# Halving the chunk of a state space kernel: from 128 tokens per tile to two chunks of 64 on the partitions of one

## The chip, the cores and the metric

The kernel runs on one core of a Trainium2 chip. The metric is the device time of one execution in microseconds (us); the figure compared is the median of several executions. Profile times are counted from the start of the profiled execution's span.

The engines are called PE (TensorE matmul), PEld (TensorE weight load, which overlaps PE), DVE (VectorE), ACT (ScalarE), POOL (GpSimd) and SP (the engine that issues most of the DMAs). "L623" is line 623 of the kernel whose profile is shown.

## The reference

Two stages. First a state space layer (Mamba-2 form) over 4 batches, 8 heads, 768 tokens, 32 features per head and a state of 16: the tokens are cut into chunks, inside a chunk the output is a masked and decayed matrix product, and between chunks a state is carried. Then a two-layer MLP with a PReLU over the 3072 tokens x 256 features, with 2048 hidden features. All in fp32 (the weights come as 64-bit floats and are converted on the chip).

```python
for c in range(nc):                                   # chunks of 32 tokens in the reference
    ...                                               # xc, Bc, Cc, la: this chunk's x, B, C, log a
    cum = np.cumsum(la, axis=-1)
    L = np.exp(cum[..., :, None] - cum[..., None, :]) * causal
    CB = np.einsum('bhin,bhjn->bhij', Cc, Bc)         # the gram
    y_intra = np.einsum('bhij,bhjd->bhid', CB * L, xc)            # "within" the chunk
    y_inter = np.einsum('bhin,bhnd->bhid', Cc, state) * np.exp(cum)[..., None]   # "across"
    y[:, :, sl] = y_intra + y_inter
    Bx = Bc (outer) xc * exp(cum_last - cum)
    state = decay_full * state + sum_j Bx             # what the chunk adds to the state
...
h = x @ w_in                                          # 3072x256 @ 256x2048
g = np.maximum(h, 0.0) + alpha * np.minimum(h, 0.0)
out = g @ w_out                                       # 3072x2048 @ 2048x256
```

The result does not depend on the chunk's length, so a kernel is free to choose it. The MLP's products are done with a seven-product block scheme (Strassen-Winograd) for all tokens but the first 512.

## The kernel before

There are 24 chunks of 128 tokens, taken two at a time: 12 "pairs". A pair is a Python generator that is advanced stage by stage between matmuls of the MLP of the token group before; two pairs make one group of 512 tokens. Every matmul's `tile_position` names the part of the 128x128 array that it uses; the numbers of rows (contraction) and columns (outputs) are those of its operands.

```python
P = 128; Q = 128                      # partitions; tokens in a chunk
...
def spread(z, k, tile=...):           # pairs 0 and 1: decays of a head to all partitions, by matmul
    ts = [tile(w) for w in range(2)]
    for q in range(4):
        for w in range(2):
            ...
            nc.tensor.matmul(ts[w][:, q * Q : (q + 1) * Q],
                             ident[rs, row : row + 1].to_broadcast([64, P]), z[rs, k], ...,
                             tile_position=(64 * w, 0))
...
def load_spread(gp, b, c):            # later pairs: the same by DMA, from a scratch in DRAM
    for k, t in enumerate(loads["p", gp][1]):          # two tiles abc, 128 x (8 heads x 128)
        rows = scratch["z", b // 2]....[b % 2, c + k]
        nc.sync.dma_start(out=t..., in_=rows.unsqueeze(0).to_broadcast([P, H, Q]))
```

The stages of a pair (cut; `k` is the chunk, `w` the half of the heads, `h` a head, `r` a group of 32 partitions of B and C, which is two heads):

```python
for i in range(2):                    # B and C turned, 4 transposes of 128x128
    for k in range(2):
        nc.tensor.transpose(tp[...], nat[:, i, k], ident)
...                                   # copied to bh and ct by ACT; cz: C with every second head zeroed
# decays inside a chunk: a scan along the row, for each of 128 start tokens
def half_decays(k, w):
    for i in range(2):                # 8 scans of 128x256 for a pair
        nc.vector.tensor_tensor_scan(out=dv[:, k, hs], data0=abc[k][:, hs],
                                     data1=ident_p[0], ...)
# pairs 0 and 1: 4 scans of 128x512 that read spread's result in PSUM
...
# what a chunk adds to the state, and the states
for k in range(nk):                   # nk = 2; 1 in the last pair of a batch
    for w in range(KC):
        nc.tensor.matmul(dps[ws, k], bn[:, k, ws], xt[:, k, w * P : (w + 1) * P],
                         tile_position=(0, 64 * w), ...)             # 128x64 of the array
for k in range(nk):
    nc.vector.scalar_tensor_tensor(out=new[:, k], in0=old, scalar=pf[...], in1=dps[:, k], ...)
...
# gram of B and C
for k in range(2):
    for r in range(4):
        nc.tensor.matmul(gram[r][:, k], bh[rs, k], cz[rs, :, k],
                         tile_position=(32 * r, 0), ...)             # 32x128, 256 columns stream
...
for r in ...:                         # times the decays: 4 of 128x512 on DVE
    nc.vector.tensor_tensor(out=dec[:, :, hs], in0=gram[r], in1=dec[:, :, hs], op=ALU.mult)
# the outputs: across (from the states) and within (from the chunk), summed in PSUM
for k in range(2):
    for w in range(KC):
        nc.tensor.matmul(y[w][:, k], st[k][ws], cd[ws, k], start=not begun, stop=False,
                         tile_position=(64 * w, 0), ...)             # 64x128, 128 columns stream
for k in range(2):
    for w in range(KC):
        for q in range(4):
            nc.tensor.matmul(y[w][32 * q : 32 * q + 32, k], xt[:, k, h * D : (h + 1) * D],
                             dec[:, k, h], start=False, stop=True,
                             tile_position=(0, 32 * q), ...)         # 128x32, 128 columns stream
for w in range(KC):
    nc.scalar.copy(out=xts[g][:, w, ...], in_=y[w]...)               # xT, the input of the MLP
```

The start (cut): the weights are loaded in 16 pieces (`raw`) and converted by ACT, POOL and DVE (`convert_a`, `convert_b`, `convert`), and the first two pairs have no MLP to hide behind.

```python
load_next(2); rows_clamp(0); ssm(0)
held["pr"] = rows_scan(0); rows_out(0)
load_pair(1); load_second(); load_next(2); load_pair(2, False); load_next(2)
load_spread(2, ...)
ssm(0); convert_a(*pieces[0]); ssm(0); convert_b(*pieces[0]); ssm(0)
convert_a(*pieces[1]); ssm(1); convert_next(halves=(nc.vector, nc.gpsimd)); ssm(0); ssm(1)
slopes(alpha)
prelus = [hidden_two(0, 0, 0, spare())]
convert_a(*pieces[2]); convert_next(first=False); ssm(1); convert_a(*pieces[3])
prelus.append(hidden_two(0, 2, 0, spare()))
for rest in prelus: rest()
convert_next(); ssm(1); convert_next(first=False)
...                                   # 4 hidden blocks of the other 256 tokens, then f = 4 to 15:
for f in range(FIRST, NF):            # pairs 2 and 3 in between, weights converted along the way
    ...
    hidden(0, f); convert_next(); output(f - FIRST)
```

Of the kernel before, what the change touches and what calls it, by code (L numbers as in the profile page):

```python
# [22 lines left out]
def kernel(  # L23
# [32 lines left out]
    P = 128  # L56
    Q = 128
    CPB = S // Q
# [27 lines left out]
    lda = ctx.enter_context(tc.tile_pool(name="lda", bufs=3))  # L86
# [45 lines left out]
    def load_spread(gp, b, c):  # L132

        for k, t in enumerate(loads["p", gp][1]):
            rows = scratch["z", b // 2].rearrange("(b h c) t -> b c h t", b=2, h=H)[b % 2, c + k]
            nc.sync.dma_start(out=t.rearrange("p (h t) -> p h t", h=H),
                              in_=rows.unsqueeze(0).to_broadcast([P, H, Q]))

    def load_pair(gp, decays=True):
# [18 lines left out]
        abc = []  # L158
# [8 lines left out]
        for k in range(2 if gp >= NB else 0):  # L167
            abc.append(lda.tile([P, H * Q], F32, name="abc"))
        loads["p", gp] = nat, abc, xt, ap
        if decays:  # L170
            load_spread(gp, b, c)
# [95 lines left out]
    def keep_warm(to, n, cols=2 * Q):  # L267

        for i in range(n):
# [6 lines left out]
    ident_h = const.tile([P, H * Q], F32, name="ident_h")  # L276
    nc.vector.tensor_copy(out=ident_h.rearrange("p (h t) -> p h t", h=H),
                          in_=ident.unsqueeze(1).to_broadcast([P, H, Q]))
# [13 lines left out]
    zeros = const.tile([P, Q], F32, name="zeros")  # L292
    nc.gpsimd.memset(zeros, 0.0)
    ends = const.tile([P, Q], F32, name="ends")
    nc.vector.memset(ends, 0.0)
    nc.vector.memset(ends[:, Q - 1 :], 1.0)
# [46 lines left out]
    def rows_scan(i):  # L343

        d0 = held[i]
        nc.vector.memset(d0[:, Q:], 0.0)
        pr = prep.tile([RW, Q], F32, name="pr")
        nc.vector.tensor_tensor_scan(out=pr[:, ::-1], data0=d0[:, 1:][:, ::-1],
                                     data1=ends[:RW, ::-1], initial=0.0,
                                     op0=ALU.mult, op1=ALU.add)  # L350
        return pr

    def rows_out(i):
# [4 lines left out]
        nc.vector.tensor_tensor_scan(out=rpf, data0=d0, data1=zeros[:RW], initial=1.0,  # L358
                                     op0=ALU.mult, op1=ALU.add)
        nc.vector.memset(d0[:, :1], 0.0)  # L360
        for key, t in (("z", d0), ("pf", rpf)):
            scratch[key, i] = dr.tile([RW, Q], F32, name=f"{key}{i}")
            nc.sync.dma_start(out=scratch[key, i], in_=t)

    def rows_turn(i, pr):
# [6 lines left out]
        nc.scalar.copy(out=t, in_=ps[:, :RW])  # L372
        if i == 0:
            nc.scalar.copy(out=alpha, in_=ps[:, RW : RW + NF])
        prt[i] = t
        return ps
# [15 lines left out]
    def first_a(ap, eng):  # L392

        z = prep.tile([P, 2, Q], F32, name="z", bufs=2)
        eng.tensor_scalar(out=z.rearrange("p k t -> p (k t)"), in0=ap, scalar1=1e-6,
                          scalar2=1.0, op0=ALU.max, op1=ALU.min)
        eng.memset(z[:, :, :1], 0.0)
        return z

    def spread(z, k, tile=lambda w: ss_tile()):  # L400

        ts = [tile(w) for w in range(2)]
        for q in range(4):
            for w in range(2):
                rs = slice(64 * w, 64 * w + 64)
                row = 64 * w + N * q
                nc.tensor.matmul(ts[w][:, q * Q : (q + 1) * Q],
                                 ident[rs, row : row + 1].to_broadcast([64, P]), z[rs, k],
                                 start=(q == 0), stop=True, tile_position=(64 * w, 0),
                                 skip_group_check=True)  # L410
        return ts
# [5 lines left out]
    def pair(gp):  # L417
# [4 lines left out]
        dec = work.tile([P, 2, H, Q], F32, name="dec")  # L422
        dv = dec.rearrange("p k h t -> p k (h t)")

        def decays(k):

            if abc:
                for w in range(2):
                    half_decays(k, w)
                return  # L430
            for w, t in enumerate(ahead.pop(k, None) or spread(z, k)):
                ws = slice(512 * w, 512 * w + 512)
                nc.vector.tensor_tensor_scan(out=dv[:, k, ws], data0=t, data1=ident_h[:, ws],
                                             initial=0.0, op0=ALU.mult, op1=ALU.add)

        def half_decays(k, w):
            for i in range(2):
                hs = slice((2 * w + i) * 2 * Q, (2 * w + i + 1) * 2 * Q)
                nc.vector.tensor_tensor_scan(out=dv[:, k, hs], data0=abc[k][:, hs],  # L439
                                             data1=ident_p[0], initial=0.0, op0=ALU.mult,  # L440
                                             op1=ALU.add)

        ahead = {}

        pf = ap
        if gp == 0:
            z = first_a(ap, nc.vector)
            ahead[0] = spread(z, 0)
            ahead[1] = spread(z, 1, bank)
            loads["z", 1] = first_a(loads["a", 1], nc.gpsimd)  # L450
            yield
            nc.vector.tensor_scalar(out=ap, in0=ap, scalar1=1e-6, scalar2=1.0, op0=ALU.max,
                                    op1=ALU.min)
            pf = prep.tile([P, 2 * Q], F32, name="pf")
            for k in range(2):
                ks = slice(k * Q, (k + 1) * Q)
                nc.vector.tensor_tensor_scan(out=pf[:, ks], data0=ap[:, ks], data1=zeros,
                                             initial=1.0, op0=ALU.mult, op1=ALU.add)
        elif not abc:
            z = loads.pop(("z", gp))  # L460
            ahead[0] = spread(z, 0, bank)
# [16 lines left out]
        def spread_c():  # L478
            for e in range(2):
                o = cz[:, e].rearrange("p k t -> p (k t)")  # L480
                if gp == 0 and e == 1:
                    nc.gpsimd.tensor_scalar(out=o, in0=ct, scalar1=par[:, e : e + 1],
                                            scalar2=None, op0=ALU.mult)
                else:
                    nc.scalar.mul(o, ct, par[:, e : e + 1])
# [5 lines left out]
        fine = gp >= 2 * GC // 2  # L491
        if not fine:
            spread_c()
        if gp == 0:
            keep_warm(rows_turn(0, held.pop("pr"))[:, HT:], 5, Q)
            yield
        bn = bns.pop(gp) if gp in bns else pair_loads(gp)
        if gp == 1:
            c_decayed()
            dps = spare()  # L500
            ahead[1] = spread(z, 1, lambda w: ss_tile())
        elif gp:
            yield

        if fine:
            for k in range(2):
                for w in range(2):
                    half_decays(k, w)
                    if k == 1 and w == 1:
                        spread_c()  # L510
                    yield
        else:
            decays(0)
            if gp:
                yield
            if gp != 1:
                decays(1)
# [4 lines left out]
        nk = 1 if last else 2  # L522
        st = [masked.get(b)]
        new = work.tile([P, 2, P], F32, name="state")
        sm = work.tile([P, 2, P], F32, name="sm")

        def added(dps):
            dps = dps.rearrange("p (k m) -> p k m", m=P)
            for k in range(nk):
                for w in range(KC):  # L530
                    ws = slice(64 * w, 64 * w + 64)
                    nc.tensor.matmul(dps[ws, k], bn[:, k, ws], xt[:, k, w * P : (w + 1) * P],  # L532
                                     start=True, stop=True, tile_position=(0, 64 * w),
# [542 lines left out]
```

## Time and profile before

The median is 378.76 us (three executions, 378.55 to 379.11); the profiled execution's span is 377.2 us, at a mean granted PE clock of 0.994.

| what, from the table of instruction groups | count | busy us |
|---|---|---|
| L741 and L766: matmuls of the MLP's seven-product part, 128x256 | 1120 | 287.2 in all |
| L561: gram (three rows: into ss, hp and bank) | 192 | 34.1 |
| L616: across, 64x128 | 80 | 10.1 |
| L623: within, 128x32 | 384 | 15.2 |
| L439: scans of later pairs on DVE, 128x256 | 80 | 48.0 |
| L433: scans of pairs 0 and 1, 128x512 | 8 | 9.4 |
| L600: decays times gram, 128x512 | 46 | 30.0 |
| abc<-z: DMAs of 512 KB, 4.9 us from issue to landing | 20 | |

How to read it: a busy time is the time in which at least one instruction of that group ran, so for PE, whose instructions overlap, it is no sum of durations, and the time a group holds the array is better read from where the next group starts in the timeline. Each fp32 matmul of the program shows as two records with a weight load each. A wait is put down to the engine whose signal came last. The granted clock is 0.8 of full speed in the second of 40 slices of the span, and 0.9 or more in all others.

### The profile page before, as it was taken

What the parts mean: (1) busy time and instruction counts of PE and PEld (TensorE: products, weight loads), DVE (VectorE), ACT (ScalarE), POOL (GpSimd) and SP (SyncE); (2) the same over time, 40 slices, a digit from 0 to 9 for tenths busy, and PEclk for the clock granted to TensorE, in tenths of its full rate; (3) what the DMA queues carried; (4) which work ended last, traced back from release to release, by engine and by line L of the source; (5) the groups of instructions that cost most, each with busy time, mean ns of one, the idle gap of its engine ahead of it and who ended that gap; (6) DMA issues with size and microseconds to landing.
All of it is one profiled execution on the core that took longest, in us unless ns stands there. A gap on an engine that the chain in (4) does not pass through costs nothing.

```text
span 377.2 us, 6178 instructions
## 1 busy us (share of the span) xinstructions
PE 367.2 (97%) x2223; PEld 295.5 (78%) x2223; DVE 241.5 (64%) x461; ACT 179.5 (48%) x384; POOL 203.2 (54%) x212
## 2 busy tenths in 40 slices
PE   7999999999999999999999999999999999999996
PEld 6767566668778788788788788888788788888884
DVE  7777699967636737747737847647856734543364
ACT  1466756525344445545435535525625525543541
POOL 4764476679766846445456345356364355254512
PEclk9899999999999999999999999999999999999999
DMA  7999697921008901001901901901711000001003
GB/s 141 186 225 346 162 272 171 180 70 56 30 0 156 179 2 54 5 0 30 180 3 30 179 2 29 180 2 28 140 44 21 9 0 15 17 0 30 1 0 83
DMA packets 121878, 30.71 MB, mean 81 GB/s; under 512 B 93736, under 2 KB 117752, under 8 KB 121848
## 3 DMA queue, kind: packets, MB, share of 16 engines
q1 hardware_dynamic: 116736, 29.74, 35.4%
q10 hardware_dynamic: 5112, 0.59, 1.1%
q8 instruction: 17, 0.28, 0.3%
q14 instruction: 13, 0.11, 0.1%
HBM read 26.98 MB, written 3.34 MB: 80 GB/s over the span
## 4 chain that ended last, share of the span: by engine, by line
PE 84%; DVE 5%; SPq 4%; DMA 2%; ACT 2%; issue 1%; ACTq 0%; POOLq 0%; DVEq 0%
PE hp L766 33%; PE bank L741 32%; PE bank L680 5%; PE hp L642 3%; PE ss L623 2%; PE ss L561 2%; SPq L165 2%; SPq L163 1%; DMA raw<-in_moe_w_in_dram 1%; PE ss L616 1%; DVE dec L439 1%; PE ss L532 1%; DMA nat<-in_B_dram 1%; PE hp L561 1%; PE hp L657 1%
## 5 line engine op out<-in xcount | busy, mean ns | idle before, releaser
L809 POOL TENSOR_TENSOR gt<-gt 128x512 f32<-128x512 f32 x58 | 73.6, 1270 | 31.8 <-DVE gt L751 24.8
L751 DVE SCALAR_TENSOR_TENSOR gt<-hp,s_mul,gt 128x256 f32<-128x256 f32 x120 | 52.5, 479 | 47.8 <-ACT gt L749 46.8
L741 PE MATMUL bank<-gt,w_out 128*128 128x256 f32 x320 | 82.5, 382 | 0.4 <-ACT o_sb L687 0.4
L749 ACT ACTIVATE gt<-hp,s_alpha 128x256 f32<-128x256 f32 x120 | 50.3, 470 | 47.2 <-PE hp L766 32.9
L741 PEld LDWEIGHTS bank<-gt,w_out 128*128 128x128 f32 x320 | 60.0, 190 | 11.2 <-issue 2.3
L800 POOL TENSOR_TENSOR gt<-gt 128x512 f32<-128x512 f32 x20 | 25.4, 1270 | 78.3 <-DVE gt L751 78.3
L741 PE MATMUL bank<-gt,ws 128*128 128x256 f32 x240 | 58.3, 379 | 0.0
L741 PEld LDWEIGHTS bank<-gt,ws 128*128 128x128 f32 x240 | 45.1, 190 | 5.8
L439 DVE TENSOR_TENSOR_SCAN dec<-abc,bank 128x256 f32<-128x256 f32 x80 | 48.0, 660 | 0.0
L766 PE MATMUL hp<-xs,w_in 128*128 128x256 f32 x160 | 42.9, 390 | 0.0
L766 PE MATMUL hp<-xT,w_in 128*128 128x256 f32 x160 | 41.9, 384 | 0.0
L766 PE MATMUL hp<-xs,ws 128*128 128x256 f32 x160 | 41.1, 379 | 0.0
L785 DVE TENSOR_TENSOR hp<-hp,u 128x512 f32<-128x512 f32 x20 | 14.0, 700 | 39.7 <-ACT u L783 39.7
L774 ACT COPY m<-hp 128x512 f32<-128x512 f32 x20 | 11.7, 586 | 51.5 <-PE hp L766 51.5
L766 PEld LDWEIGHTS hp<-xs,w_in 128*128 128x128 f32 x160 | 28.7, 189 | 7.7 <-issue 3.3
L766 PEld LDWEIGHTS hp<-xs,ws 128*128 128x128 f32 x160 | 30.4, 190 | 4.1
L766 PEld LDWEIGHTS hp<-xT,w_in 128*128 128x128 f32 x160 | 29.7, 190 | 5.0 <-issue 1.4
L680 PEld LDWEIGHTS bank<-w_out,gt 128*128 128x128 f32 x128 | 24.2, 190 | 9.6 <-issue 5.4
L680 PE MATMUL bank<-w_out,gt 128*128 128x256 f32 x128 | 30.6, 381 | 0.6 <-POOL w_out L261 0.6
L789 DVE TENSOR_TENSOR c<-hp,m 128x512 f32<-128x512 f32 x20 | 13.6, 681 | 19.3 <-PE hp L766 19.3
L642 PE MATMUL hp<-xT,w_in 128*128 128x512 f32 x48 | 23.2, 605 | 0.0
L783 ACT COPY u<-hp 128x512 f32<-128x512 f32 x20 | 11.7, 585 | 23.0 <-PE hp L766 23.0
(155 smaller groups left out, 557.1 us busy)
## 6 DMA issues: line engine op xcount, KB each, us to landing
abc<-z SPq DMA_DIRECT2D x20, 512.0 KB, 4.9
raw<-in_moe_w_in_dram SPq DMA_DIRECT2D x8, 512.0 KB, 5.5
raw<-in_moe_w_out_dram SPq DMA_DIRECT2D x8, 512.0 KB, 6.8
xt<-in_x_dram SPq DMA_DIRECT2D x24, 128.0 KB, 3.3
out_dram<-o_sb SPq DMA_DIRECT2D x32, 64.0 KB, 1.9
nat<-in_B_dram SPq DMA_DIRECT2D x22, 64.0 KB, 2.7
nat<-in_C_dram SPq DMA_DIRECT2D x22, 64.0 KB, 3.5
ap<-pf SPq DMA_DIRECT2D x11, 128.0 KB
```

Of the source, the lines that this page charges most:

```text
L439: nc.vector.tensor_tensor_scan(out=dv[:, k, hs], data0=abc[k][:, hs], data1=ident_p[0], initial=0.0, op0=ALU.mult, op1=ALU.add)
L642: nc.tensor.matmul(hp, w_in[:, k, f * P : (f + 1) * P], xts[g][:, k], start=(k == 0), stop=(k == KC - 1))
L680: nc.tensor.matmul(pos[0][t // 2][:, t % 2], gt[:, t * Q : (t + 1) * Q], w_out[:, f], start=(f == 0 and t % 2 == 0), stop=(f == NF - 1), s ...
L741: nc.tensor.matmul(ms[g][i][:, h], w, blocks[g, z][n][:, p], start=(q == 0 and h == 0), stop=(q == NQ - 1), skip_group_check=True)
L749: nc.scalar.mul(o[:, p], h[:, p], s_alpha[:, fs[p]])
L751: nc.vector.scalar_tensor_tensor(out=o[:, p], in0=h[:, p], scalar=s_mul[:, fs[p]], in1=o[:, p], op0=ALU.mult, op1=ALU.max)
L766: nc.tensor.matmul(to[:, p], w(2 * z + p), b, start=start and p == 0, stop=True, skip_group_check=True)
L774: nc.scalar.copy(out=m1, in_=A)
L785: nc.vector.tensor_tensor(out=Y, in0=Y, in1=u2, op=ALU.add)
L789: nc.vector.tensor_tensor(out=c22, in0=A, in1=m5, op=ALU.add)
L800: nc.gpsimd.tensor_tensor(out=tc_, in0=g22, in1=g12, op=ALU.subtract)
L809: eng.tensor_tensor(out=o, in0=x0, in1=x1, op=ALU.subtract)
```

## The change

A chunk becomes 64 tokens long (`L`), and two chunks (`e` = 0, 1) lie on the 128 partitions of a tile, so a pair of tiles now holds four chunks. What was one 128x128 block of decays and gram per head and tile becomes two blocks of 64x64, one above the other: half of the elements. The gram then uses 32x64 parts of the array and the within products 64x32 parts, eight at a time instead of four; there are four states per pair instead of two. Across and within no longer sum in PSUM: within is copied by ACT, and DVE adds across to it. The decays of later pairs are loaded as one DMA of 256 KB per tile with runs of 2 KB, and their scans halve. The start is ordered anew, pairs 0 and 1 lose an ACT copy and a POOL product, and piece 0 of the weights is finished on DVE alone.

```diff
+    L = Q // 2
 def load_spread(gp, b, c):
-        for k, t in enumerate(loads["p", gp][1]):
-            ...
-            nc.sync.dma_start(out=t..., in_=rows.unsqueeze(0).to_broadcast([P, H, Q]))
+        t = loads["p", gp][1]
+        for k in range(2):
+            rows = scratch["z", b // 2].rearrange("(c e) x -> c e x", e=2)[c + k]
+            rows = rows[:, b % 2 * H * L : (b % 2 + 1) * H * L]
+            nc.sync.dma_start(out=t[:, k], in_=rows.unsqueeze(1).to_broadcast([2, L, H * L]))
 def spread(z, ...):                                  # 64x64 parts, 64 columns, both chunks at once
+        for i in range(8):
+            for e in range(2):
+                for w in range(2):
+                    nc.tensor.matmul(ts[w][es, i * L : (i + 1) * L], ...,
+                                     tile_position=(64 * w, e * L))
 def half_decays(k, w):                               # 4 scans of 128x256 for a pair
-            for i in range(2):
-                nc.vector.tensor_tensor_scan(out=dv[:, k, hs], data0=abc[k][:, hs], ...)
+            nc.vector.tensor_tensor_scan(out=dec[:, w, k]..., data0=abc[:, k, ...], ...)
 # pairs 0 and 1: 2 scans of 128x512
 def added(dps):                                      # two banks, 64x64 parts
-                nc.tensor.matmul(dps[ws, k], bn[:, k, ws], xt[:, k, w * P : (w + 1) * P],
-                                 tile_position=(0, 64 * w), ...)
+                for e in range(2 if 2 * k + 1 < nk else 1):
+                    nc.tensor.matmul(dps[e][ws, k], bn[es, k, ws],
+                                     xt[es, k, w * P : (w + 1) * P],
+                                     tile_position=(e * L, 64 * w), ...)
 def states(dps):
-            for k in range(nk):                      # nk = 2, or 1
+            for i in range(nk):                      # nk = 4, or 3
 def products_bc():
-                    nc.tensor.matmul(gram[r][:, k], bh[rs, k], cz[rs, :, k],
-                                     tile_position=(32 * r, 0), ...)
+                for e in range(2):
+                    for r in range(4):
+                        nc.tensor.matmul(gram[r][es, k], bh[rs, k, es], cz[rs, :, k, es],
+                                         tile_position=(32 * r, e * L), ...)
 # 4 products of decays and gram, now of 128x256 each
 # outputs
-                    nc.tensor.matmul(y[w][:, k], st[k][ws], cd[ws, k], start=not begun, ...)
+        for i in range(first, 4):                    # four states; 64 columns stream
+            for w in range(KC):
+                nc.tensor.matmul(across[w][:, i * L : (i + 1) * L], st[i][ws],
+                                 cd[ws, k, e * L : (e + 1) * L],
+                                 tile_position=(64 * w, 0), ...)
-                    nc.tensor.matmul(y[w][32 * q : 32 * q + 32, k], xt[:, k, ...],
-                                     dec[:, k, h], tile_position=(0, 32 * q), ...)
+                    for e in range(2):
+                        nc.tensor.matmul(within[e][32 * q : 32 * q + 32, w, k],
+                                         xt[es, k, h * D : (h + 1) * D], dec[es, w, k, q],
+                                         tile_position=(e * L, 32 * q), ...)
-            nc.scalar.copy(out=xts[g][:, w, ...], in_=y[w]...)
+        for e in range(2):
+            nc.scalar.copy(out=to...[:, :, :, e], in_=within[e])
+        for w in range(KC):
+            nc.vector.tensor_tensor(out=to[:, w, first * L :], in0=across[w][:, first * L :],
+                                    in1=to[:, w, first * L :], op=ALU.add)
 # order of the stages of later pairs: added and states come before the scans
 # order of the start
+    ssm(1); ssm(0); ssm(0); slopes(alpha); convert_a(*pieces[0]); ssm(1); ssm(0)
+    convert_a(*pieces[1]); convert_b(*pieces[0]); ssm(0)
+    convert_next(halves=(nc.vector,)); ssm(1)
     prelus = [hidden_two(0, 0, 0, spare())]
+    convert_next(first=False); ssm(1); convert_a(*pieces[2]); convert_a(*pieces[3])
     prelus.append(hidden_two(0, 2, 0, spare()))
+    prelus[0](); convert_b(*pieces[2]); prelus[1]()
     convert_next(); ssm(1); convert_next(first=False)
```

## The prediction

> **What bounds the kernel now.** I read the page first: shares of the engines and the makeup of the chain that ended last.
>
> ```profile
> PE 367.2 (97%) x2223; PEld 295.5 (78%) x2223; DVE 241.5 (64%) x461; ACT 179.5 (48%) x384; POOL 203.2 (54%) x212
> ...
> PE 84%; DVE 5%; SPq 4%; DMA 2%; ACT 2%; issue 1%; ACTq 0%; POOLq 0%; DVEq 0%
> ```
>
> PE ends last nearly everywhere; DVE, which the change relieves most, has a third of the span to spare. So a step counts in full only if it shortens what PE runs, and DVE's relief counts only where PE stands and waits for DVE. The timeline of PE shows where that is: after 30 us only three waits of more than 0.4 us remain, all before 61 us.
>
> ```profile
> 43.79 1.99 PE L680 MATMUL bank<-w_out,gt 128*128 128x256 f32 x8 [0.58 <-POOL w_out L261]
> ...
> 50.91 0.48 PE L561 MATMUL ss<-cz,bc 32*128 32x256 f32 x1 [0.48 <-DVE state L544]
> ...
> 60.01 0.34 PE L616 MATMUL bank<-cd,sm 64*128 64x128 f32 x1 [0.45 <-DVE dec L600]
> ```
>
> From there to the end PE is fed without a break, so the price of a pair is what its matmuls hold of PE. The timeline of PE for one pair, narrowed to across and within, then of the pair before it for what it adds to the state:
>
> ```profile
> 222.08 0.71 PE L616 MATMUL ss<-cd,sm 64*128 64x128 f32 x8
> 222.72 1.08 PE L623 MATMUL ss<-dec,xt 128*32 128x128 f32 x32
> 223.74 0.48 PE L766 MATMUL hp<-xs,w_in 128*128 128x256 f32 x1
> ```
>
> ```profile
> 68.75 0.66 PE L532 MATMUL ss<-xt,bn 128*64 128x128 f32 x8
> 69.34 0.70 PE L642 MATMUL hp<-xT,w_in 128*128 128x512 f32 x1
> ```
>
> A group's price is start to next start: across 0.64, within 1.02, added 0.59 us. The same for the gram, 72.98 to 74.05 in that timeline, is 1.07, and for the transposes 0.44 (201.21 to 201.65). Sum 3.76. As a test: in the chain of waits "PE ss L623 x32" stands at 136.51 and, six pairs on, at 308.90, so 28.7 us apart; the two quads of MLP between them cost 24.4 without a pair (12.2 each, from 322.19 to 334.42 in the same chain). A pair costs some 4.3 us of PE; the rest is the switch back to the MLP.
>
> The start is another matter. Its chain of waits (the first 62 us):
>
> ```profile
> 23.84 4.92 DMA raw<-in_moe_w_in_dram
> ...
> 28.83 0.69 ACT wt L218
> 29.52 0.60 ACT wg L225
> 30.12 0.28 ACT xT L630
> ...
> 30.44 3.73 PE hp L657 x16
> ...
> 42.39 2.33 DVE dec L439 x4
> ```
>
> The first 30 us end with a weight piece that lands at 28.75; ACT, in order, converts it, and only then copies pair 1's xT, for which PE waits. The 40s are DVE: the scans of pair 2.
>
> **What the Trainium skill says.** "TensorE: Matmul & The Clock Gate", LDWEIGHTS: a load takes its number of columns divided by 1.2 GHz, whatever the rows, so an estimate of 107 ns for 128 columns, 53 for 64, 27 for 32. The trace agrees: in pair 1's across (28.44 to 28.89, two row tiles at a time) a second load starts 0.11 us after the first, and the next matmul only 0.11 us later. Same page, Part 3 "The mechanism": tiles with other positions run at once, started some 4 ns apart; here the four gram tiles start at 72.98 to 73.00, a little slower, some 7 ns each. "FP8 and Floating Point Precision", TensorE Precision Notes: true fp32 is four passes; with two records per matmul here each record is two passes, and at the full clock of 2.4 GHz that the first page gives, 128 columns make 107 ns, which is the spacing of the rounds below. "TensorEngine Tiling (Array Packing)", Key Properties: changing the tiling mode drains the array; the trace agrees, a new group starts some 0.1 us after the stream of the last round has ended (28.88 plus 0.11, then 29.09), and its first round takes twice as long (28.44 to 28.66).
>
> **The change on PE, group by group.** These are the rounds in pair 1 (PE's timeline):
>
> ```profile
> 28.66 0.27 PE L616 MATMUL ss<-cd,sm 64*128 64x128 f32 x1
> 28.77 0.27 PE L616 MATMUL bank<-cd,sm 64*128 64x128 f32 x1
> ...
> 29.33 0.40 PE L623 MATMUL ss<-dec,xt 128*32 128x128 f32 x8
> 29.55 0.40 PE L623 MATMUL bank<-dec,xt 128*32 128x128 f32 x8
> ```
>
> Across: a round of 2 tiles each 0.11 us. Within: 8 records, two rounds of 4 tiles, each 0.22 us. A round is the longer of the stream and the weight load of one tile, and at least 7 ns per tile.
> - Transposes: unchanged.
> - Added: 8 records in 4 rounds become 16 in 4 rounds (4 tiles). Same 128 columns. 0.
> - Gram: 16 records of 256 columns, 4 tiles, 4 rounds of 0.215, become 32 of 128 columns, 8 tiles, 4 rounds of 0.11 (loads of 64 columns hide; 8 x 7 = 56 ns of issue too). It becomes the shape of added: 1.07 to 0.59, -0.48.
> - Across: 8 records in 4 rounds become 16 in 8 (four states). The stream halves to 53 ns but the load of 128 columns stays 107, so rounds stay 0.11: +0.43. In the first pair of a batch 2 rounds become 6, the same.
> - Within: 32 records, 8 rounds of 0.11, become 64 of 64 columns with 8 tiles, 8 rounds of 0.057: -0.42.
> - The mode switches stay as many.
>
> Sum per pair -0.47 us. Pairs 2 to 11 run inside the stream that PE bounds: 10 x -0.47 = -4.7 us.
>
> **DVE.** Per pair: scans 8 to 4, twice 2.33 to twice 1.16 (row above): -2.3. Gram products 4 x 0.68 become 4 x 0.42 (the duration of a 128x256 product that reads PSUM, group L830): -1.0. Two more states at 0.34: +0.7. Two adds of across at 0.42: +0.85. Net -1.8. Only in the 40s and 50s does PE wait for this: each of two loop turns loses 1.16 us of scans, so the waits at 50.91 and 60.01 and smaller ones near them go, an estimated -1.1. The one at 43.79 comes before the scans, from ACT's queue, and stays.
>
> **The start.** DVE needs 2.3 us less of scans for each of pairs 0 and 1 (4 x 1.17 to 2 x 1.17), spreading takes half as long, and xT of pair 0 should come some 2 us sooner. But the order of instructions on ACT and SP is the same where it counts: the same weight piece is issued after the same loads, lands at about 28.7, is converted on ACT (1.3 us), then come two copies (0.65) and now, before PE can go, a DVE add (0.42 and the hand-over). PE goes on at 31.3 instead of 30.44: +0.85.
>
> Sum: -4.7 - 1.1 + 0.85 = -4.95, so 378.76 becomes 373.8; I say 374.0.
>
> **The rivals.**
> 1. Eight tiles don't run at once (four do, or the issue of 128 records with loads takes 13 ns each). Then gram and within gain nothing and across still loses 0.43: 10 x 0.43 - 1.1 + 0.85 = +4, about 383. For it: no group of the kernel before uses eight tiles. Against: the four gram tiles at 72.98 go 7 ns apart and leave the issue idle for the rest of a 215 ns round, and at 50.05 the second passes of two tiles ran while a third waited for a signal, so the overlap is not a fixed pattern of four.
> 2. Across is not held by its loads: two loads with other row groups already go side by side, and if a third could be ahead, rounds fall to 0.057 and across stays 0.64. Then -9 us in all, about 369.5. Against it: 28.56 to 28.66, where a matmul waits for its own load and nothing else.
> 3. The start is freed more than I think: the decays' DMA halves (512 to 256 KB per chunk pair, runs of 512 B to 2 KB) while DMA is at 0.83 of its time between 30 and 62 us, and the order of the start is new. If the weight piece landed earlier by its share, up to 3 us more: 371. Against: that piece is queued ahead of the first decays.
> 4. A new wait in the steady part: added now needs two PSUM tiles and comes right after the transposes, and xT ends with DVE instead of ACT, some 0.9 us later, with the token sums of POOL behind it. In the timeline at 194 to 204 us POOL's sums had 0.95 us to spare before its next product, and ACT's copy of the transposes ended at 202.8, 0.6 us before added would start. Tight but enough; if not, 0.3 us per pair, +3: 377.
>
> **Range and chances.** The middle is 374.0. Rivals 2 and 3 pull to 369.5, rival 4 to 377; rival 1, at one in ten, lies outside. I take 369.5 to 378.5. Faster by over 2% means below 371.2: only with rival 2 or a much better start, 0.2. Within 2%: 0.75. Slower by over 2%: 0.05, since even rival 1 gives +1%.
>
> **What would show it.** In the profile after: gram's start to next start near 0.6, within near 0.6, across near 1.07; 8 starts within 60 ns in gram and within; pairs 28.25 us apart instead of 28.7; PE's waits at 50 and 60 us gone; the block of hidden matmuls that stood at 30.44 at about 31.3, released by DVE. It is wrong if within keeps 1 us, if PE shows new waits at added or at across after 100 us, or if the main loop starts much before 34 us.

## The result: 6% slower

The changed kernel takes 401.58 us (median of four executions, 401.11 to 402.56), the kernel before beside it 378.65 us. The ratio is 1.061, with an interval of 1.058 to 1.063. The prediction said 374.0 us and gave 369.5 to 378.5 as its range.

In the page of the changed kernel, these are the lines of busy shares, of the granted PE clock in 40 slices, of the makeup of the chain that ended last, and of the decay loads:

```profile
PE 371.5 (93%) x3057; PEld 297.9 (75%) x3057; DVE 223.0 (56%) x470; ACT 178.0 (45%) x379; POOL 206.4 (52%) x209
...
PEclk9986996699999999999999999999999999999999
...
PE 73%; DVE 7%; DMA 5%; issue 5%; SPq 4%; ACT 2%; POOL 2%; POOLq 0%; ACTq 0%; DVEq 0%
...
abc<-z SPq DMA_DIRECT2D x20, 256.0 KB
```

DVE got its relief (241.5 to 223.0 us), but PE's busy time grew by 4 us instead of shrinking, and its share of the span fell from 97 to 93%. The clock is down to 0.6 in three of the first eight slices (a slice is 10 us), and DMA and "issue" have grown in the chain. So most of the loss is in the first 80 us: across of the third pair starts at 78.19 instead of 60.01. PE's timeline there has two long waits:

```profile
33.30 6.72 PE L656 MATMUL hp<-xT,w_in 128*128 128x256 f32 x16 [4.97 <-DVE xT L629]
...
71.50 1.09 PE L476 MATMUL bank<-ident,nat 128*128 128x128 f32 x4 [10.26 <-issue]
72.38 3.62 PE L641 MATMUL hp<-xT,w_in 128*128 128x512 f32 x4
```

The first row is the block that stood at 30.44 before and took 3.72 us for the same 16 matmuls: it comes 2.9 us later and takes 3.0 us longer. The second is the transposes of the fourth pair, which started at 55.52 without a wait. The third takes 3.62 us where the same block took 1.88. Each wait is thus paid twice, in idle time and then in matmuls at half the clock (the table of windows gives a granted clock of 0.50 from 33 to 39 us and from 64 to 76).

What ACT and DVE waited for, in their timelines of the changed kernel:

```profile
31.03 0.66 ACT L220 ACTIVATE wt<-raw 128x512 f32<-128x512 f32 x1 [4.37 <-DMA raw<-in_moe_w_in_dram]
...
44.21 0.67 ACT L220 ACTIVATE wt<-raw 128x512 f32<-128x512 f32 x1 [1.41 <-DMA raw<-in_moe_w_in_dram]
```

```profile
69.44 0.22 DVE L345 TENSOR_SCALAR r<-rows 96x128 f32<-96x128 f32 x1 [6.98 <-DMA rows<-in_a_dram]
...
70.67 0.40 DVE L591 TENSOR_TENSOR dec<-ss,dec 128x256 f32<-128x256 f32 x1
70.99 0.41 DVE L591 TENSOR_TENSOR dec<-bank,dec 128x256 f32<-128x256 f32 x1
```

Weights and rows come late. The last row explains a wait that the view calls only "issue": the transposes write `bank`, which this gram product still reads, and the product stands in DVE's queue behind the rows. They start 0.1 us after it ends.

The loads are late in two different ways. SP issues its loads in order; from its timeline:

```profile
25.93 0.58 SPq L204 DMA_DIRECT2D raw<-in_moe_w_in_dram  x1
...
27.07 1.08 SPq L139 DMA_DIRECT2D abc<-z  x2
28.26 4.31 SPq L204 DMA_DIRECT2D raw<-in_moe_w_in_dram  x1
...
54.87 1.20 SPq L139 DMA_DIRECT2D abc<-z  x2
56.11 2.85 SPq L123 DMA_DIRECT2D rows<-in_a_dram  x1
```

The piece that ACT takes up at 31.03 was issued ahead of the decay loads (`abc`) and was there 5.1 us later, as before (4.92): it is late only because it was issued 2.1 us later. The piece that ACT takes up at 44.21 and the rows were issued right behind decay loads and needed 16 and 13 us.

What holds up these two shows in the table of windows. Its last columns are PE clock, share of the 16 DMA engines, and GB/s. First the changed kernel, then the kernel before:

```profile
31.00:32.00 1.00, 0.00 (x0) 0.00 (x0) 0.00 (x0) 0.97 (x2) 0.22 (x1) 1.00 0.18 70
32.00:33.00 1.00, 0.00 (x0) 0.00 (x0) 0.18 (x1) 0.79 (x3) 0.39 (x1) 0.79 0.14 53
...
42.00:43.00 1.00, 1.00 (x6) 0.88 (x5) 0.90 (x2) 0.81 (x2) 0.61 (x1) 1.00 0.13 49
...
46.00:47.00 1.00, 1.00 (x7) 0.84 (x5) 0.00 (x0) 1.00 (x3) 0.38 (x1) 1.00 0.13 51
```

```profile
31.00:32.00 1.00, 1.00 (x6) 0.90 (x5) 0.99 (x1) 0.00 (x0) 1.00 (x1) 1.00 1.18 348
32.00:33.00 1.00, 1.00 (x7) 0.87 (x6) 0.58 (x1) 0.53 (x2) 0.92 (x2) 1.00 1.06 319
```

While weight pieces are outstanding, the changed kernel falls again and again to some 50 GB/s at a share of 0.13. That is two engines of sixteen (0.125). The Trainium skill states the reason: "DMA: Bandwidth & Descriptors", Rules for kernel authors, says that an outermost dimension smaller than 16 confines a DMA to at most that many engines. The new decay load reads a source of [2, 64, 512]; the old one's was [128, 8, 128]. My reading, then, is that half the bytes on an eighth of the engines take longer, and that loads issued behind them, which need all sixteen, end only when those two engines get to their share.

### The profile page after: what moved, and what is told of

The parts are those of the page before. It is cut to its first block, busy times and chain, and to the rows that moved or that the text cites. A ratio compares the mean times of both kernels' runs of the same rounds, so it can differ in the third digit from the quotient of the medians. Undisturbed runs are those within 1.5% of the kernel's fastest.

```text
span 399.7 us, 7827 instructions
## 1 busy us (share of the span) xinstructions
PE 371.5 (93%) x3057; PEld 297.9 (75%) x3057; DVE 223.0 (56%) x470; ACT 178.0 (45%) x379; POOL 206.4 (52%) x209
## 4 chain that ended last, share of the span: by engine, by line
PE 73%; DVE 7%; DMA 5%; issue 5%; SPq 4%; ACT 2%; POOL 2%; POOLq 0%; ACTq 0%; DVEq 0%
PE hp L765 29%; PE bank L740 26%; PE bank L679 5%; DMA raw<-in_moe_w_in_dram 5%; PE hp L641 4%; DVE gt L750 4%; PE ss L608 2%; SPq L167 2%; PE ss L617 2%; ACT gt L748 2%; PE ss L522 1%; SPq L165 1%; PE hp L556 1%; DVE dec L442 1%; DMA ap<-in_a_dram 1%
## 5 line engine op out<-in xcount | busy, mean ns | idle before, releaser
L740 PEld LDWEIGHTS bank<-gt,w_out 128*128 128x128 f32 x320 | 60.0, 190 | 10.1 <-issue 1.2
L765 PE MATMUL hp<-xT,w_in 128*128 128x256 f32 x160 | 42.7, 389 | 0.1
L765 PEld LDWEIGHTS hp<-xs,w_in 128*128 128x128 f32 x160 | 28.7, 189 | 6.6 <-ACT u L782 2.2
L641 PE MATMUL hp<-xT,w_in 128*128 128x512 f32 x48 | 25.0, 646 | 1.0 <-DVE gt L645 1.0
L442 DVE TENSOR_TENSOR_SCAN dec<-abc,bank 128x256 f32<-128x256 f32 x40 | 25.9, 672 | 0.0
L750 DVE SCALAR_TENSOR_TENSOR gt<-c,s_mul,gt 128x256 f32<-128x256 f32 x40 | 20.9, 563 | 0.0
```

Of the source, the lines that this page charges most:

```text
L442: nc.vector.tensor_tensor_scan(out=dec[:, w, k].rearrange("p q t -> p (q t)"), data0=abc[:, k, w * 4 * L : (w + 1) * 4 * L], data1=ident_p ...
L641: nc.tensor.matmul(hp, w_in[:, k, f * P : (f + 1) * P], xts[g][:, k], start=(k == 0), stop=(k == KC - 1))
L740: nc.tensor.matmul(ms[g][i][:, h], w, blocks[g, z][n][:, p], start=(q == 0 and h == 0), stop=(q == NQ - 1), skip_group_check=True)
L750: nc.vector.scalar_tensor_tensor(out=o[:, p], in0=h[:, p], scalar=s_mul[:, fs[p]], in1=o[:, p], op0=ALU.mult, op1=ALU.max)
L765: nc.tensor.matmul(to[:, p], w(2 * z + p), b, start=start and p == 0, stop=True, skip_group_check=True)
```

## The experiments

Line numbers differ by up to four between these kernels (L617, L618 and L621 are all "within").

**The decay loads on 16 engines.** Same bytes, same number of transfers, cut by half of the partitions instead of by chunk:

```diff
-        for k in range(2):
-            rows = scratch["z", b // 2].rearrange("(c e) x -> c e x", e=2)[c + k]
+        for e in range(2):
+            rows = scratch["z", b // 2].rearrange("(c e) x -> e c x", e=2)[e, c : c + 2]
             rows = rows[:, b % 2 * H * L : (b % 2 + 1) * H * L]
-            nc.sync.dma_start(out=t[:, k], in_=rows.unsqueeze(1).to_broadcast([2, L, H * L]))
+            nc.sync.dma_start(out=t[e * L : (e + 1) * L],
+                              in_=rows.unsqueeze(0).to_broadcast([L, 2, H * L]))
```

> The changed kernel with its decay loads cut by half-tile (64 partitions, leading dimension 64) instead of by chunk (leading dimension 2); the bytes, the number of transfers and everything else are as in the changed kernel. Theory (two-engine transfers hold up every later load): the transfers take near 5 us each as before the change, the transposes of the second pair start without their 10 us wait, the clock stays near 0.99, and the time falls by 20 to 27 us, to 374 to 381 us. Rival A (the new order of the start and the longer write of z hold the loads up, not the number of engines): less than 5 us come back, 396 us or more. Rival B (the throttle lowers the clock because of the new matmul forms): clock stays at 0.97 and the time near 400 us.

Measured: 392.22 us, ratio 1.037 (1.034 to 1.039). A transfer takes 4.1 us from issue to landing. 9.4 us came back: more than rival A allowed, less than half of what I expected. Both long waits of PE are still there, 5.9 us at 32.10 and 4.6 us at 62.96. For the first this fits the order of issue above: its piece does not stand behind the decay loads.

**The kernel before with two-engine loads, and its control.** z is written twice; each load reads one copy for each half of the partitions, or, in the control, one copy for all of them:

```diff
+        for u in range(2):
+            nc.sync.dma_start(out=scratch["z", i][u * CPB : (u + 1) * CPB]..., in_=d0)
-            nc.sync.dma_start(out=t..., in_=rows.unsqueeze(0).to_broadcast([P, H, Q]))
+            nc.sync.dma_start(out=t, in_=rows.unsqueeze(1).to_broadcast([2, P // 2, H * Q]))
 # control: rows of copy 0 alone, in_=rows.unsqueeze(0).to_broadcast([P, H * Q])
```

> The kernel before with two copies of z in DRAM, each decay load reading one copy for each half of the partitions, so that its leading dimension is 2; one small write more. Nothing else of the change is in it. Theory (two-engine transfers are the loss): these loads move twice the bytes of the changed kernel's on two engines, so the loss is at least as large as there: 15 to 45 us slower than before, 394 to 424 us, with waits for the raw weights and the B and C tiles and a clock under 0.98. Rival A (the loss needs the change's order of the start or its matmuls): within 2 us of before, 377 to 381 us.

> The control for the kernel before with two-engine loads: the same two copies of z in DRAM, the same layout and runs, but each decay load reads one copy for all 128 partitions, so that its leading dimension is 128. Theory (the number of engines is the loss): within 2 us of the kernel before, 376.5 to 380.5 us. Rival (the extra write or the new layout of z is what cost): 390 us or more.

Measured: 414.61 us on two engines, ratio 1.096 (1.093 to 1.099); the control 379.45 us, ratio 1.002 (0.999 to 1.005). The same stretch in the table of windows, two engines first, then the control:

```profile
31.00:33.00 2.00, 2.00 (x11) 1.77 (x10) 0.18 (x1) 0.83 (x2) 1.92 (x2) 1.00 0.13 53
```

```profile
31.00:33.00 2.00, 2.00 (x11) 1.77 (x10) 1.15 (x2) 0.84 (x2) 1.83 (x3) 1.00 0.92 334
```

Nothing else of the change is in this pair of kernels (one half of the partitions reads the second copy, that is all), and the leading dimension alone costs 35 us. So the leading dimension, and with it the number of engines, is shown as a cause. Two waits of PE stand out, 16.9 and 16.1 us long. The start near 30 us is not among them: xT of the second pair keeps PE waiting 1.4 us there. These loads carry twice the changed kernel's bytes, so the size does not transfer.

**Where the other waits come from: the order on ACT, and the order of the gram products.** Both on top of the spread loads. In the first, the two copies that make xT of the second pair no longer stand in ACT's queue behind the fifth weight piece. In the second, the gram product whose bank the next pair's transposes get is taken second instead of last.

```diff
-    convert_next()                       # with convert_a(*pieces[4]) on ACT
+    convert_next(first=False)
     ssm(1)
+    convert_a(*pieces[4])
```

```diff
-... (2, 3, 0, 1) if fine else (3, 2, 1, 0) if gp > 1 else range(4)
+... (2, 3, 0, 1) if fine else (3, 0, 2, 1) if gp > 1 else range(4)
```

> On top of the decay loads spread over 16 engines: the ScalarE step of the fifth weight piece moves behind the two copies of the second pair's outputs. Theory (the outputs stand in ScalarE's queue behind a piece that is still on its way, and the idle that follows lets the clock drop): the 16 hidden matmuls start at about 27.5 us instead of 32.1 and take 3.7 us instead of 6.6; 5 to 8 us less than that run, 384 to 387 us. Rival (the weights' arrival sets the pace in any order, so the earlier start is given back before 60 us): 390 us or more.

> On top of the decay loads spread over 16 engines: of the four gram products of the third and fourth pair the one that frees the bank which the next pair's transposes are given is taken second instead of last. Theory (the transposes near 58 us wait for a bank whose last reader stands behind the scan of the second rows tile on VectorE): the 4.6 us wait ahead of the transposes goes and the hidden matmuls after them take 1.9 instead of 3.6 us; 5 to 7 us less than that run, 385 to 387.5 us. Rival (the same wait comes back at the next use of the products, the state term of the third pair): 390 us or more.

> Both changes of order together, on the decay loads spread over 16 engines. Theory: they add, as they lie at different places: 10 to 15 us less than the spread alone, 377 to 382 us. Rival (the weights' arrival): the second gains little once the first has moved the work up, 385 us or more.

Measured: ACT's order 388.08 us, ratio 1.024 (1.021 to 1.026); the products' order 387.10, 1.021 (1.019 to 1.024); both 382.09, 1.008 (1.005 to 1.010). With ACT's order the 16 hidden matmuls start at 27.14 us and take 3.72. The order gave 4.1 us rather than 5 to 8; the next block now stands 2.1 us for DVE. With the products' order the transposes start at 58.81 without a wait; the two rows, of PE's timeline with the spread alone and then with the new order:

```profile
62.96 1.08 PE L477 MATMUL bank<-ident,nat 128*128 128x128 f32 x4 [4.60 <-issue]
```

```profile
58.81 0.60 PE L477 MATMUL bank<-ident,nat 128*128 128x128 f32 x4
```

4.1 and 5.1 us singly, 10.1 together: they add, and neither was given back to the arrival of weights. (The kernel before beside these three had a median of 378.53, beside the spread alone 378.04, so each of these gains is uncertain by some 0.5 us.) The buffer wait is new with the change. Added now takes two tiles out of a rotation of three, so the transposes that used to get an `ss` tile get the bank that is freed last.

**The idle and the clock.** Again on the spread loads: warming matmuls fill the wait near 30 us, nothing is moved.

```diff
+    warmed = spare()
+    keep_warm(warmed, 24)
```

> On top of the decay loads spread over 16 engines: 24 more warming matmuls in TensorE's idle stretch near 26 to 32 us, nothing moved. Theory (the idle itself lowers the clock, and the 16 hidden matmuls that follow pay for it): they start at 32 us as without, but take 3.7 us instead of 6.6; 2 to 3.5 us less, 388.5 to 390.5 us. Rival (the matmuls are slow for another reason than the idle): 392 us, no change.

Measured: 394.48 us, ratio 1.041 (1.038 to 1.045), above what was expected and above the rival too. The total says nothing, since 24 calls are 48 records and took 10.6 us, so that the hidden matmuls start 4.5 us later than without them. The rows of PE's timeline settle the question all the same; first with the spread alone, then with the warming:

```profile
32.10 6.54 PE L657 MATMUL hp<-xT,w_in 128*128 128x256 f32 x16 [5.88 <-DVE xT L630]
```

```profile
26.09 10.63 PE L273 MATMUL hp<-warm 128*128 128x256 f32 x48
36.56 3.62 PE L657 MATMUL hp<-xT,w_in 128*128 128x256 f32 x16
```

The same 16 matmuls take 3.62 us without the idle. So the idle is what slows them, not the new forms of matmul (rival B of the first run). How long an idle it takes, the runs do not settle. "TensorE: Matmul & The Clock Gate", Part 1 of the Trainium skill, gives an idle window of about 3.4 us after which the clock is halved. Idle of 4.97 and 5.88 us was followed by half speed and the 1.18 us that ACT's order leaves in the same place was not, which agrees. But in the next place, near 33 us, 2.08 us with ACT's order cost nothing and 2.24 us in a later run (early B tile, below) was followed by half the clock, 0.50 from 35 to 38 us. PE's timelines, ACT's order first:

```profile
33.38 1.96 PE L642 MATMUL hp<-xT,w_in 128*128 128x512 f32 x4 [2.08 <-DVE gt L669]
35.17 1.89 PE L680 MATMUL bank<-w_out,gt 128*128 128x256 f32 x8
```

```profile
33.57 2.52 PE L642 MATMUL hp<-xT,w_in 128*128 128x512 f32 x4 [2.24 <-DVE gt L669]
35.88 3.06 PE L680 MATMUL bank<-w_out,gt 128*128 128x256 f32 x8
```

Here the measurement decides: an idle well under 3.4 us was followed by half the clock too.

**Two engines once more, with both orders mended.**

```diff
 # the changed kernel with the two edits of order above; load_spread as the change has it
```

> The changed kernel with both changes of order, its decay loads as the change has them, on two engines. Theory (the two-engine loads hold up weights and tiles whatever the order of the other engines): it stays 6 to 12 us above the same orders with the loads spread, 388 to 394 us. Rival (the loads hurt only through the two orders that are mended here): within 2 us of it, 380 to 384 us.

Measured: 397.44 us, ratio 1.050 (1.047 to 1.053). The orders alone give 4.1 us, and spreading the loads on top of them gives 15.3, more than the 6 to 12 expected. PE's waits, in all, times and longest, show where the loss has moved:

```profile
PE hp L641 <- DVE gt L645: 8.9, 1, 8.9
PE ss L608 <- DVE dec L591: 4.9, 1, 4.9
```

Behind the first of them is the weight piece that was issued right behind the decay loads, at 28.40 here and at 27.81 with both orders and spread loads. In the timelines of ACT, on two engines and then spread:

```profile
45.10 0.66 ACT L220 ACTIVATE wt<-raw 128x512 f32<-128x512 f32 x1 [9.67 <-DMA raw<-in_moe_w_in_dram]
```

```profile
36.01 0.67 ACT L221 ACTIVATE wt<-raw 128x512 f32<-128x512 f32 x1 [1.44 <-DMA raw<-in_moe_w_in_dram]
```

From issue to use it takes 16.7 us against 8.2. The rival falls. The loads hold up what is issued behind them whatever the order; only the place of the wait changes.

**The steady part.** With both orders mended and the loads spread, the kernel is 2.6 us ahead of the kernel before at the fourth pair's transposes (52.87 against 55.52) and yet ends behind it. Three edits, the first on top of the two orders, the other two each on top of the first:

```diff
+        if f == 14:
+            bns[4] = pair_loads(4)          # early B tile
```

```diff
 # scans one place earlier: (0,0) and (0,1) together, then (1,0), then (1,1); none in the last place
-            for k in range(2):
-                for w in range(2):
-                    half_decays(k, w); ...; yield
+            half_decays(0, 0); half_decays(0, 1); yield
+            half_decays(1, 0); yield
+            half_decays(1, 1); spread_c(); yield
+            yield
```

```diff
 # added last: behind the scans again
+            for k in range(2): ...          # the four half_decays
             states(added([ss_tile() for e in range(2)]))
             c_decayed()
             yield
```

> On top of the spread loads and both changes of order: the weighted B tile of the fifth pair, which the added term now needs at once, is made on GpSimd two output blocks earlier, ahead of the sums of the tokens. Theory (the added term moved ahead of the scans meets a tile that was free of waits before the change): the 1.5 us wait of TensorE near 84 us goes; 1 to 1.8 us less, 380 to 381 us. Rival (GpSimd's chain of token sums is what TensorE waits for there): no change, 382 us.

> On top of the run with the early B tile: in the steady part the four decay scans of a pair go one place earlier, so that none stands ahead of the PReLU step whose bank the gram is given. Theory (the gram's rounds are fast enough, but wait some 0.4 us per pair for that step): the gram takes 0.8 us instead of 1.2 from start to next work, 7 pairs; 2 to 3 us less than the run with the early B tile, 377 to 379 us, no slower than the kernel before. Rival (the scan is hidden and the gram waits for the ScalarE half of the PReLU): under 0.7 us less.

> On top of the run with the early B tile: in the steady part the added term and the state updates go back behind the scans, where they were before the change. Theory (its old place filled a TensorE wait of 0.2 us for a ScalarE copy, but now four state updates instead of two stand ahead of the PReLU step that frees the gram's bank): the copy's wait goes, the gram's wait grows by some 0.7 us; 1 to 4 us more than the run with the early B tile. Rival (moving the added term was what cost the steady part): 2 us or more less than it.

Measured: early B tile 381.15 us, ratio 1.006 (1.003 to 1.009); scans earlier 378.74, 1.000 (0.995 to 1.005); added last 378.09, 0.999 (0.996 to 1.002). The first is undecided: its wait of 1.5 us is gone, but another near 33 us grew from 1.1 to 2.2 in that profile and was followed by half the clock, as shown above, and the intervals overlap. The two of its executions with a clock of 0.999 took 380.55 and 380.88 us, the profiled one (0.995) and another (0.997) 381.43. The second did what it was made for. Waits of PE's weight loads in the steady part, in us, times and longest, with the early B tile, then with the scans earlier:

```profile
PEld hp L766 <- ACT hp L795: 2.8, 7, 0.4
PEld hp L557 <- DVE gt L751: 2.6, 7, 0.8
```

```profile
PEld hp L769 <- ACT hp L798: 2.8, 7, 0.4
...
PEld hp L557 <- DVE gt L754: 0.2, 1, 0.2
```

In the third my expectation was wrong. The ACT wait is gone, as expected, but the gram's wait did not grow, and the rival's 2 us and more came:

```profile
PEld hp L557 <- DVE gt L751: 2.2, 7, 0.5
```

So moving added ahead of the scans did cost: from its old place it had filled PE's wait for an ACT copy. Not all of the 3.1 us is due to it: in the profiles 1.4 us are there before 55 us (the fourth pair's transposes start at 52.80 instead of 54.16), which is the clock that the profile of the early B tile lost.

**The last wait of the start.** On top of added last, the ACT step of the fifth piece moves behind the early hidden blocks:

```diff
-    convert_a(*pieces[4])
     convert_next(first=False)
     for rest in [hidden_two(0, f, 2 * Q, spare()) for f in range(0, FIRST, 2)]:
         rest()
+    convert_a(*pieces[4])
```

> On top of the run with the added term back behind the scans: the ScalarE step of the fifth weight piece moves once more, behind the PReLU of the 16 early hidden matmuls. Theory (ScalarE still stands waiting for that piece near 30 us, so the PReLU that frees the first hidden bank comes late and TensorE waits 1.6 us near 33 us): that wait goes, 1 to 1.6 us less, 376.5 to 377.2 us, just faster than the kernel before. Rival (the time is given back before 60 us, where the weights' conversion on GpSimd sets the pace): 378 us, as without.

Measured: 379.07 us (six executions), ratio 1.002 (0.999 to 1.005). The rival was right: PE's wait of 1.6 us near 33 us is gone, and at 40.35 there is one of 2.0. No version tried beats the kernel before.

## Why the prediction was wrong

**The step that failed: rival 3 and the start.** The prediction treated the decay loads as relief: "the decays' DMA halves (512 to 256 KB per chunk pair, runs of 512 B to 2 KB)". It counted bytes and runs and not engines. Spreading the loads over 16 engines is worth 9.4 us as the change stands and 15.3 us with the orders mended. No line of the sum had a term for it, and the "slower" chance of 0.05 rested on its absence.

**"The same weight piece ... lands at about 28.7" and "PE goes on at 31.3 instead of 30.44: +0.85".** The mechanism was right: ACT in order, two copies, then a DVE add, PE released by DVE. But the piece was issued at 25.93 instead of 23.84 us and ACT got it at 31.03, so PE went on at 33.30. The engines of the decay loads have no part in this: the piece was issued at 25.01 to 26.39 us in all eleven profiled kernels with chunks of 64, on two engines or sixteen, and at 23.45 to 23.84 in the three with chunks of 128. What in the change delays it stays open. What I did not see is that the faster pair 1 makes the wait longer. Before, PE was busy with across and within until 30.2 and stood 0.27 us; now it had nothing left after some 28.3, and 5 us of idle cost 3.0 us more in clock. ACT's order alone gave back 4.1 us.

**"The waits at 50.91 and 60.01 ... go, an estimated -1.1".** They went, and a much longer one took their place, for a bank that the gram now frees last: 10.26 us in the changed kernel, 4.60 with spread loads, 0 with another order of the products (5.1 us of the time). Rival 4 looked for new buffer waits only "in the steady part".

**PE group by group.** Rivals 1 and 2 fell, as expected: in pair 1 the first eight records of within start between 27.30 and 27.34 us, and across keeps its rounds of 0.11. In the changed kernel's timeline of PE:

```profile
214.28 1.11 PE L608 MATMUL ss<-cd,sm 64*128 64x64 f32 x16
215.32 0.86 PE L617 MATMUL ss<-dec,xt 64*32 64x64 f32 x64
216.11 0.70 PE L765 MATMUL hp<-xs,w_in 128*128 128x256 f32 x2
```

Start to next start, averaged over the pairs of the steady part in the timelines of PE, in us:

| group | before | predicted | changed | scans earlier |
|---|---|---|---|---|
| added | 0.50 | no change | 0.60 | 0.60 |
| gram | 1.30 | -0.48 | 1.18 | 0.87 |
| across | 0.59 | +0.43 | 0.98 | 0.98 |
| within | 1.01 | -0.42 | 0.79 | 0.79 |
| sum | 3.40 | -0.47 | 3.55 | 3.24 |

Across and the unhindered gram came out as worked out (+0.39, -0.43), though gram's base of 1.07 was that of an early pair and too low. Within was mis-sized: eight tiles do run at once, but 64 records take 0.79 us, not 0.60, so half of its gain is missing. In pair 1 of the changed kernel, where the starts can be told apart, the first 32 keep the pace that was worked out (27.30 to 27.53), and the other 32 start from 27.56 to 28.06. Added costs 0.1 on average because the last pair of a batch had one state, half the rounds, and now has three; I had it only from an early pair (0.59, as it still is there). So the groups alone allow -0.16 per pair, not -0.47. The changed kernel does not get even that. The chain of waits of the changed kernel, six pairs apart:

```profile
156.29 1.04 PE ss L608 x16
...
330.47 1.04 PE ss L608 x16
```

29.03 us per pair, against 28.73 before and 28.25 predicted. Of these 0.30 us, 0.15 are the sum of the table. The rest is the ACT wait of the weight loads, 0.4 us per pair there: with added last, where it is gone and gram still takes 1.17, a pair is 0.16 shorter. The same chain with the scans earlier and with added last:

```profile
135.56 1.04 PE ss L612 x16
...
308.20 1.04 PE ss L612 x16
```

```profile
133.56 1.04 PE ss L609 x16
...
306.77 1.04 PE ss L609 x16
```

28.77 and 28.87 us per pair: no version has a shorter pair than the kernel before. Rival 4 had this size ("0.3 us per pair, +3: 377") but named the wrong waits. In the gram it is DVE's queue that holds: in the timelines of the changed kernel, DVE first, then PE,

```profile
235.92 0.68 DVE L442 TENSOR_TENSOR_SCAN dec<-abc,bank 128x256 f32<-128x256 f32 x1
236.51 0.85 DVE L750 SCALAR_TENSOR_TENSOR gt<-hp,s_mul,gt 128x256 f32<-128x256 f32 x2
```

```profile
237.08 0.66 PE L556 MATMUL hp<-cz,bc 32*64 32x128 f32 x2
237.43 0.33 PE L556 MATMUL ss<-cz,bc 32*64 32x128 f32 x2
```

the scan delays the PReLU step that ends at 237.36, and the gram's next rounds, which write the tile that step had read, start only then, at about 237.4.

**The account.** From 401.6 us: spread loads -9.4, the two orders -10.1, then about -3.4 (early B tile and scans earlier) or -4.0 (early B tile and added last). That ends at 378 to 379, even with the kernel before, whose median was 378.04 to 378.87 beside these runs, so that each step is uncertain by some 0.5 us. The split between loads and orders depends on which is mended first (15.3 and 4.1 the other way round).

What stays open: why the unhindered gram takes 0.87 us in the steady part and 0.62 in pair 1 (22.85 to 23.47 in the changed kernel); the kernel before has the same difference (1.30 and 1.08), so it does not come with the new tiles. Also why the second half of within is slower than the first, why the piece at 25.93 is issued late, and what the scans one place earlier and added last would give together. None of these was tried by itself.

## What to carry to other kernels

Read a changed DMA by its outermost dimension before its bytes: half the bytes on two engines held up the loads issued behind it, and the profile shows that as a flat DMA share (0.13 is two of sixteen) while other engines wait for other tensors. When PE gets faster in a stage that something else ends, look at how long it will stand: idle stretches of 5 us were paid a second time in the clock here, and one of 2.24 us too. When a stage takes one more tile from a rotation, follow who gets which tile afterwards; the wait appears at an instruction the change never touched.

## What the runs showed of the hardware

Two engines moved 49 to 53 GB/s together, at a share of 0.13; in the same stretch near 32 us all sixteen moved 319 and 348 GB/s in the kernel before and 334 in the control (0.92 to 1.18). Eight small matmuls at once did not shorten a group as their columns say: 64 records of 64 columns took 0.79 us where 32 of 128 columns took 1.01. A stretch of about 5 to 6 us in which TensorE stood made the next 16 matmuls take 6.5 to 6.7 us instead of 3.6 to 3.7, and filling that stretch with idle matmuls restored them in full. A stretch of 2.24 us was followed by a clock of 0.50 in one profile; stretches of 2.08 us and less in the same place in four others were not.
